# GateLoop attention and a gated layer on one core: scores, states' sums and value products of two chunks grouped by kind, and a guard's ScalarE part behind x's upper half

## The chip, the cores and the metric

The kernel runs on one core of a Trainium2 chip. The metric is the time of one execution on the device, in microseconds (us); lower is better. The core has engines that work side by side, each in the order of its own queue: TensorE (PE in the profile; PEld is its loading of weights), VectorE (DVE), ScalarE (ACT), GpSimd (POOL) and SyncE (SP, which here only issues DMAs).

## The reference

For each of 4 batches and 8 heads a complex state of 48 x 48 runs through 768 time steps; the output of each step is the query times the state's real part. The outputs of all heads are put side by side to x (3072 tokens x 384), and x goes through a layer of width 2048.

```python
mag = np.sqrt(a_re * a_re + a_im * a_im)
scale = np.minimum(mag, 0.999) / (mag + 1e-06)
a_re_n, a_im_n = (a_re * scale, a_im * scale)
for t in range(S):
    new_re = ar * S_re - ai * S_im            # ar, ai: step t of a_re_n, a_im_n
    new_im = ar * S_im + ai * S_re
    kv = np.einsum('bhd,bhe->bhde', k[:, :, t], v[:, :, t])
    S_re, S_im = (new_re + kv, new_im)
    y[:, :, t] = np.einsum('bhd,bhde->bhe', q[:, :, t], S_re)
...
h = x @ w_in
g = h * np.cos(h)
return (g @ w_out).astype(np.float32)
```

q, k, v, a_re and a_im have the shape (4, 8, 768, 48); w_in is 384 x 2048 and w_out 2048 x 384. All is float32.

## The kernel before, in words

The recurrence is computed in chunks of 128 steps. The gates' logarithms and angles are summed up within a chunk by matmuls with triangular matrices (`lgs` for the logarithms, `phs` for the angles); keys and queries are turned and scaled by them (`ks`, `qs`; transposed they are `kT`, `qT`). Then a chunk needs three kinds of matmul: the scores `sc` (keys by queries, 8 heads, in two halves), which VectorE multiplies by a causal mask into `atm`; the chunk's own contribution to the state, `sp` (values by keys), from which VectorE makes the next chunk's `state` in two steps (`state<-sp,state`, then `state<-state,end`; at the start of a batch one step, `state<-sp,end`); and the value products `yp`, which add `atm` times values and `state` times queries. ScalarE copies `yp` to `yT`, from where x goes to memory and comes back as `xT`.

The 24 chunks are taken in 12 groups g0 to g11 of two chunks. A batch has three groups, so g3, g6 and g9 begin a batch (chunk 1 has no state to read) and g2, g5, g8 and g11 end one (their chunk 2 makes no state). The main loop runs over the groups from g2 on; one turn, a stage here, does the attention of group n, the preparation of gates, keys and queries for group n+1, the hidden layer of group n (`hp`, `hb`: x by w_in, with the cosine on ScalarE and products on VectorE into `gate`), and the products with w_out of group n-1 (`sum`, `op`; VectorE makes combinations of gates, `s` and `t_s` tiles, for them, and `ot` collects the output). For some of the w_in tiles x is split in an upper and a lower part: `xh` (ScalarE, `x_halves.upper`), `xl` and `xx` (VectorE, `lower` and `apart`).

A stage's order is written by a function `weave`. Each entry is a list of steps with two numbers, and the steps are emitted in the order of numbers spread evenly between the two:

```python
weave((mixes(n - 1, 1, 2), 0.0, 0.08), (logs(n + 1), 0.0, 0.02), (chunks(n), 0.0, 0.36),
      ...
      (products(n - 1, 1, 2), 0.05, 0.24), ...
```

The matmuls keep the order in which they are emitted; each is chained to the one before. The vector and scalar operations of the stages are then placed by a scheduler when the kernel is built, so their order in the queues follows from the emitted order and from what they need. `behind(a, b)` forbids that a is placed ahead of b. PSUM tiles of the kinds `sc`, `sp`, `yp`, `lgs`, `phs` and `hb` share five buffers.

`chunks(n)` emits for each chunk in turn the scores, the state's sums and its steps (`f_state`), and the value products (`f_out`); in the middle of chunk 2's `f_out` stands a call, `between`, that emits the matmuls `lgs` of the next group (`prods`). Behind chunk 2 come the store of x, loads of `im` and `v` and x's transposed load. `products(n-1, 1, 2)` are the `op` matmuls of one part of the group before. `guard` looks, on ScalarE, at pieces of the raw weights that POOL's queue fetches into the places of `kT` and `qT` (tile `raw`): an Abs, then a Relu with an accumulated sum; two guards run in each stage from g3 on, and each stands behind the last scalar operation emitted so far (`tail["scalar"]`).

In the profile almost all matmuls carry the line of one helper (L692), and most vector and scalar operations that of a wrapper (L681); L712 is a helper for ScalarE's function calls, L733 the one that makes `hi`, the upper part of a float.

Of the kernel before, what the change touches and what calls it, by code (L numbers as in the profile page):

```python
# [18 lines left out]
AF = mybir.ActivationFunctionType  # L19
# [468 lines left out]
def fast_path(ctx, tc, q, k, v, a_re, a_im, moe_w_in, moe_w_out, out, least, odd, wide,  # L488
# [11 lines left out]
    NCH = S // C  # L500
    G = 2
    N = B * NCH
    NG = N // G
# [30 lines left out]
    late = {}  # L534
    tail = {}
# [7 lines left out]
    def behind(ins, other):  # L543
        tc.add_manual_dep(ins.ins, other.ins.name, mybir.DependencyInfo(
            mybir.DependencyClass.NoSync, mybir.DependencyReason.DATA))
# [82 lines left out]
    def fetched(src, home=None):  # L628
        _, a, b = src.shape
        pool, tag = (ft, home) if home else (stage["pool"], "raw")  # L630
        raw = pool.tile([C, a, b], I64, tag=tag, name="raw", bufs=stage["bufs"])
        chain(nc.gpsimd.dma_start(out=raw, in_=src), "gpsimd")
        words = raw.rearrange("p a b -> p (a b)").bitcast(U32).rearrange(
            "p (a b two) -> p a b two", a=a, two=2)
        return words[:, :, :, 0], words[:, :, :, 1]
# [9 lines left out]
        yield  # L645
        vector.tensor_tensor(out=bits, in0=bits, in1=lo, op=ALU.add)

    def guard(src, home):

        _, e = fetched(src, home)
        bits = e.bitcast(F32)
        behind(scalar.activation(out=bits, in_=bits, func=AF.Abs), tail["scalar"])
        scalar.activation(out=bits, in_=bits, func=AF.Relu, scale=-1.0, bias=least_e_b,
                          accum_out=odd[:, ds(next(odds), 1)])

# [368 lines left out]
    def f_scores(n, hh):  # L1026
        y, (g, i) = Y[n], divmod(n, G)
        if i == 0 and hh == 0:
            X[g]["atm"] = ft.tile([C, G, H, C], F32, tag="atm", name="atm", bufs=1)
        y["atm"] = X[g]["atm"][:, i]  # L1030
        ps = pa.tile([C, HH, C], F32, tag="a", name="sc")
        for h in range(HH):
            head = hh * HH + h
            matmul(ps[:, h], lhsT=X[n // G]["kT"][:, n % G * H + head],
                   rhs=queries(n, head), start=True, stop=True)
        y["masked"] = vector.tensor_tensor(
            out=y["atm"][:, ts(hh, HH)], in0=ps, in1=causal.unsqueeze(1).to_broadcast([C, HH, C]), op=ALU.mult)
        if "whole" in X[n // G - 1]:
            behind(y["masked"], X[n // G - 1]["whole"])

    def f_out(n, between=lambda: None):
        y, (g, i) = Y[n], divmod(n, G)
        vals = X[g]["v"][:, i]
        state = y.get("state")
        if i == 0:
            X[g]["yT"] = ft.tile([C, HH, G, C], F32, tag="yT", name="yT", bufs=1)
        ps = pa.tile([C, HH, C], F32, tag="a", name="yp")
        for p in range(HH):
            if p == (0 if n % NCH < NCH - 1 else 2):
                between()  # L1050
            for side in range(2):
                matmul(ps[ds(side * 64, D), p], lhsT=vals[:, 2 * p + side],
                       rhs=y["atm"][:, 2 * p + side], start=True, stop=(state is None))
            if state is not None:
                for side in range(2):
                    matmul(ps[ds(side * 64, D), p], lhsT=state[:, 2 * p + side],
                           rhs=queries(n, 2 * p + side), start=False, stop=True)
        for side in range(2):
            half = ds(side * 64, D)
            copied = scalar.copy(out=X[g]["yT"][half, :, i], in_=ps[half])  # L1060
            if g >= PEG:
                behind(copied, late["upper"])
# [58 lines left out]
    def f_state(n):  # L1121
        if n % NCH < NCH - 1:
            state_sums(n)
            for _ in state_next(n):
                pass

    def f_x(g, i=0, n=G):

        if i == 0:
            X[g]["moved"] = rows_d.tile([HH, 2, D, G, C], F32, tag="x", name="x")  # L1130
        for side in range(2):
            late["x"] = nc.sync.dma_start(
                out=X[g]["moved"][:, side, :, ds(i, n)].rearrange("p d g t -> d p g t"),
                in_=X[g]["yT"][ds(side * 64, D), :, ds(i, n)])
# [47 lines left out]
    def x_halves(g):  # L1182

        x = X[g]

        def all_of():
            return x["xT"].rearrange("p c g t -> p (c g t)")

        def upper():
            for name, tag in ("xx", "lg"), ("xh", "lo"), ("xl", "rs"):  # L1190
                x[name] = gt.tile([C, G * DM], F32R, tag=tag, name=name)

            scalar.activation(out=x["xh"], in_=all_of(), func=AF.Copy, scale=1.0 - 2.0 ** -13)

        def lower():
            rest_ = vector.tensor_tensor(out=x["xl"], in0=all_of(), in1=x["xh"].bitcast(F32),
                                         op=ALU.subtract)
            if g + 1 < NG:
                behind(rest_, X[g + 1][BEFORE])

        def apart():
            x["apart"] = vector.scalar_tensor_tensor(
                out=x["xx"], in0=x["xl"].bitcast(F32), scalar=-SHIFT,
                in1=x["xh"].bitcast(F32), op0=ALU.mult, op1=ALU.add)

        return upper, lower, apart
# [226 lines left out]
    def mixes(g, lo, hi):  # L1433
        return [lambda p=p: mixed(g, p) for p in range(lo, hi)] if g >= PLAIN else []
# [34 lines left out]
    def prods(g):  # L1469
        return powers(g) if 0 <= g < NG else []  # L1470
# [11 lines left out]
    def logs(g):  # L1482
        yield from each(g_log, g)
# [7 lines left out]
    def phases(g):  # L1491
        return [lambda i=i: g_phase(g, i) for i in range(G)] if 0 <= g < NG else []

    def chunks(g):
        for n in range(g * G, g * G + G):
            for hh in range(2):
                yield lambda n=n, hh=hh: f_scores(n, hh)
            yield lambda: None
            yield lambda n=n: (f_state(n), f_out(n, lambda: n % G and [t() for t in prods(g + 1)]))
        yield lambda: (f_x(g), g + 2 < NG and load(g + 2, ("im",), put=after_x), f_xt(g))  # L1500
        if PEG < g + 1 < NG:
            yield lambda: (ends(g + 1), load(g + 1, ("v",), put=lambda **kw: behind(
                nc.sync.dma_start(**kw), late["ends"])))
        if g + 2 < NG:
            late["next"] = [lambda: load(g + 2, ("k", "q"), put=turned_first)]
# [29 lines left out]

    def guarded(homes):

        for home, _ in zip(homes, list(guards)):
            yield lambda home=home: guard(guards.pop(0), home)

    into, back = weight_parts()
    guards = [src for _, src in into + back if src.dtype != F32]
# [277 lines left out]
    for n in range(2, NG):  # L1820
        turned_keys, plain = list(keys(n + 1)), n == PLAIN
        split = x_halves(n) if any(three(n, jp) for jp in THREE) else ()
        guard_ = list(guarded(("kT", "qT"))) if n > 2 else []
        convert = [lambda jp=jp: halves(jp) for jp in THREE if FROM[jp] == n + 1]
        weave((mixes(n - 1, 1, 2), 0.0, 0.08), (logs(n + 1), 0.0, 0.02), (chunks(n), 0.0, 0.36),
              (upper[2:] if plain else [], 0.0, 0.2), (products(n - 1, 0, 1), -0.02, -0.01),
              (products(n - 1, 1, 2), 0.05, 0.24), (products(n - 1, 2, 3) if n < NG - 1 else [], 0.28, 0.36),
              (mixes_again(n - 1, "s3"), 0.06, 0.18), (mixes_again(n - 1, "s2"), 0.19, 0.27),
              (angles(n + 1), 0.2695, 0.2699), (carries(n + 1), 0.336, 0.34), (second(n - 1, 1), 0.36, 0.5),
              (mixes_again(n - 1, "s4"), 0.37, 0.48),  # L1830
              (products(n - 1, 2 + (n < NG - 1), 7), 0.4, 0.56),
              (convert[0:-2], 0.76, 0.76), (convert[-2:], 0.76, 0.98),
              (phases(n + 1), *((0.472, 0.476) if plain else (0.476, 0.484))),
              (turned_keys[0:1], 0.5, 0.5), (split[0:1], *[0.54 if n < NG - 1 else 0.525] * 2), (turned_keys[1:2], 0.53, 0.53),
              (turned_keys[2:3], 0.56, 0.56), (turned_keys[3:4], 0.6, 0.6), ([lambda: rest_of(n - 1)], 0.605, 0.605), (split[1:2], *[0.542 if n < NG - 1 else 0.53] * 2),
              (split[2:3], *[0.544 if n < NG - 1 else 0.54] * 2), ([lambda: p_end(n + 1, 0, G)] if n + 1 < NG else [], 0.615, 0.615), (last_quarter() if plain else [], 0.9, 1.0), (first(n), 0.56, 1.0),
              (mixes(n, 0, 1), 0.98 if convert else 0.92, 1.0 if n < NG - 1 else 0.97), (guard_[0:1], 0.47, 0.47),
              (guard_[1:2], 0.505, 0.505))
    checked = verdict(late, temp)

    def judged():
# [99 lines left out]
```

## Time and profile before

| | before |
|---|---|
| median of 3 runs | 629.77 us (629.24 to 630.23) |
| profiled execution, whole | 629.86 us |
| its span in the profile | 628.1 us, 12990 instructions |
| PE busy | 608.1 us (97%) |
| PEld busy | 555.3 us (88%) |
| DVE busy | 531.8 us (85%) |
| ACT busy | 461.3 us (73%) |
| POOL busy | 28.5 us (5%) |
| DMA | 95.04 MB, mean 151 GB/s |

The span is what the engines' records cover; about 1.8 us of the execution lie outside it. Busy shares are averages over the whole span: what an engine's wait costs is read in the stage where it stands. A row of the timeline gives the start in us, the duration, engine, line, operation, `out<-in`, shapes and the number of records run together (a matmul in this number format leaves two records; `x16` is eight matmuls); in square brackets stands the idle time before it and what ended that. Neighbouring operations of an engine overlap at their edges, so what one costs in a row of them is read from start to start.

### The profile page before, as it was taken

What the parts mean: (1) busy time and instruction counts of PE and PEld (TensorE: products, weight loads), DVE (VectorE), ACT (ScalarE), POOL (GpSimd) and SP (SyncE); (2) the same over time, 40 slices, a digit from 0 to 9 for tenths busy, and PEclk for the clock granted to TensorE, in tenths of its full rate; (3) what the DMA queues carried; (4) which work ended last, traced back from release to release, by engine and by line L of the source; (5) the groups of instructions that cost most, each with busy time, mean ns of one, the idle gap of its engine ahead of it and who ended that gap; (6) DMA issues with size and microseconds to landing.
All of it is one profiled execution on the core that took longest, in us unless ns stands there. A gap on an engine that the chain in (4) does not pass through costs nothing.

```text
span 628.1 us, 12990 instructions
## 1 busy us (share of the span) xinstructions
PE 608.1 (97%) x5057; PEld 555.3 (88%) x5057; DVE 531.8 (85%) x779; ACT 461.3 (73%) x832; POOL 28.5 (5%) x45
## 2 busy tenths in 40 slices
PE   8899999999999998998999999999999999999995
PEld 5788867776889998998999999998999999999995
DVE  6999989967898799899889989889889989982471
ACT  7888687286698597698598698598599598572440
POOL 4010110000000000000000000000000000000000
PEclk9999999999999999999999999999999999999999
DMA  9969574714937567486396496496496494371001
GB/s 235 257 185 226 166 214 79 201 46 107 226 69 187 152 148 202 125 180 176 102 223 179 111 220 175 105 218 166 121 222 174 110 228 125 104 176 52 27 0 32
DMA packets 237569, 95.04 MB, mean 151 GB/s; under 512 B 209501, under 2 KB 229726, under 8 KB 237498
## 3 DMA queue, kind: packets, MB, share of 16 engines
q1 hardware_dynamic: 229960, 68.51, 46.5%
q0 software_dynamic: 5824, 25.50, 13.1%
q8 instruction: 42, 0.69, 0.5%
q10 hardware_dynamic: 1714, 0.11, 0.2%
q14 instruction: 29, 0.24, 0.1%
HBM read 69.28 MB, written 24.81 MB: 150 GB/s over the span
## 4 chain that ended last, share of the span: by engine, by line
PE 55%; ACT 19%; DVE 13%; issue 5%; DMA 4%; SPq 2%; ACTq 0%; DVEq 0%
PE hp L692 20%; PE op L692 13%; PE sum L692 12%; PE hb L692 3%; ACT xT L681 2%; PE yp L692 2%; DVE tr L681 2%; PE phs L692 2%; ACT tan L712 2%; ACT rs L712 2%; ACT gate L712 2%; DMA kT<-moved 2%; ACT L708 2%; ACT lg L712 2%; DVE gate L681 2%
## 5 line engine op out<-in xcount | busy, mean ns | idle before, releaser
L712 ACT ACTIVATE gate<-hp,half_pi_b 128x512 f32<-128x512 f32 x96 | 68.7, 715 | 50.2 <-PE hp L692 30.3
L692 PE MATMUL hp<-xT,w_in 128*128 128x256 f32 (+1 forms) x492 | 104.9, 369 | 0.0
L692 PE MATMUL op<-w_out,gate 128*128 128x192 f32 (+1 forms) x464 | 102.3, 370 | 0.0
L692 PEld LDWEIGHTS hp<-xT,w_in 128*128 128x128 f32 x492 | 89.7, 190 | 12.6 <-issue 0.2
L692 PEld LDWEIGHTS op<-w_out,gate 128*128 128x128 f32 x464 | 78.7, 190 | 15.2 <-issue 0.4
L692 PE MATMUL hp<-xh,wh 128*128 128x256 f32 x342 | 60.8, 286 | 0.0
L681 ACT ACTIVATE xT<-hp 128x512 bf16<-128x512 f32 x96 | 60.0, 625 | 0.0
L692 PE MATMUL hp<-xl,wl 128*128 128x256 f32 x342 | 59.0, 281 | 0.0
L692 PE MATMUL sum<-w_out,gate 128*128 128x192 f32 x304 | 52.5, 326 | 0.0
L681 DVE SCALAR_TENSOR_TENSOR gate<-hp,gate 128x512 f32<-128x512 f32 x57 | 39.2, 688 | 13.0 <-ACT xT L681 12.7
L692 PE MATMUL sc<-qT,kT 96*128 96x128 f32 x384 | 49.6, 278 | 0.3 <-ACT qT L681 0.3
L692 PEld LDWEIGHTS hp<-xh,wh 128*128 128x128 f32 x342 | 49.5, 189 | 0.5
L692 PEld LDWEIGHTS sc<-qT,kT 96*128 96x128 f32 x384 | 46.7, 192 | 3.2 <-issue 1.9
L692 PEld LDWEIGHTS sum<-w_out,gate 128*128 128x128 f32 x304 | 49.5, 190 | 0.1
L692 PE MATMUL hb<-xx,wx 128*128 128x256 f32 x342 | 48.6, 282 | 0.0
L692 PEld LDWEIGHTS hp<-xl,wl 128*128 128x128 f32 x342 | 48.4, 188 | 0.0
L681 DVE TENSOR_TENSOR hp<-hp,gate 128x512 f32<-128x512 f32 x57 | 39.3, 693 | 6.8 <-PE hp L692 2.6
L692 PEld LDWEIGHTS hb<-xx,wx 128*128 128x128 f32 x342 | 44.0, 188 | 0.0
L681 ACT ACTIVATE gate<-hb 128x512 f32<-128x512 f32 x57 | 35.8, 628 | 10.8 <-PE hb L692 9.8
L692 PE MATMUL yp<-atm,v 128*48 128x128 f32 x352 | 33.8, 278 | 3.4 <-DVE atm L681 3.4
L681 DVE TENSOR_TENSOR gate<-hp,gate 128x512 f32<-128x512 f32 x39 | 26.2, 678 | 12.8 <-ACT xT L681 12.6
L681 DVE TENSOR_TENSOR atm<-sc,causal 128x512 f32<-128x512 f32 x48 | 32.3, 683 | 4.8 <-PE sc L692 4.8
(161 smaller groups left out, 1222.2 us busy)
## 6 DMA issues: line engine op xcount, KB each, us to landing
moved<-tr SPq DMA_DIRECT2D x20, 768.0 KB
raw<-in_moe_w_in_dram POOLq DMA_DIRECT2D x16, 768.0 KB, 5.7
raw<-in_moe_w_out_dram POOLq DMA_DIRECT2D x16, 768.0 KB, 5.3
kT<-moved SPq DMA_DIRECT2D x80, 96.0 KB
qT<-moved SPq DMA_DIRECT2D x20, 384.0 KB
k<-in_k_dram SPq DMA_DIRECT2D x24, 192.0 KB
q<-in_q_dram SPq DMA_DIRECT2D x24, 192.0 KB
v<-in_v_dram SPq DMA_DIRECT2D x24, 192.0 KB
```

Source lines behind the costliest of these rows:

```text
L681: ins = getattr(self.engine, op)(**kw)
L692: chain(nc.tensor.matmul(out, **kw), "tensor")
L708: chain(nc.scalar.preload_act_table_set(table))
L712: chain(nc.scalar.activation(func=func, **kw))
```

## The change

`chunks(n)` is split into four entries: `scores(n)` for both chunks, then `states(n)` for both, then `outs(n)` (value products of both, then the x store, the `im` loads and x's transposed load), and later `fetches(n)` (`v` and `k`, `q` loads). The call in the middle of `f_out` is gone, and `prods(n+1)` has an entry of its own. `products(n-1, 1, 2)` has a narrower place. `guard` is split into the raw piece's fetch and the ScalarE part; the second guard's ScalarE part now stands behind `xh`, and the fetches and ScalarE parts have a place each. The number of matmuls, vector and scalar operations and loads is the same.

```diff
-    def guard(src, home):
-        _, e = fetched(src, home)
+    def guard(raw, other):
+
+        _, e = raw
         bits = e.bitcast(F32)
-        behind(scalar.activation(out=bits, in_=bits, func=AF.Abs), tail["scalar"])
+        behind(scalar.activation(out=bits, in_=bits, func=AF.Abs), other)
...
-    def f_out(n, between=lambda: None):
+    def f_out(n):
...
-            if p == (0 if n % NCH < NCH - 1 else 2):
-                between()
...
-            scalar.activation(out=x["xh"], in_=all_of(), func=AF.Copy, scale=1.0 - 2.0 ** -13)
+            late["xh"] = scalar.activation(out=x["xh"], in_=all_of(), func=AF.Copy,
+                                           scale=1.0 - 2.0 ** -13)
...
-    def chunks(g):
-        for n in range(g * G, g * G + G):
-            for hh in range(2):
-                yield lambda n=n, hh=hh: f_scores(n, hh)
-            yield lambda: None
-            yield lambda n=n: (f_state(n), f_out(n, lambda: n % G and [t() for t in prods(g + 1)]))
+    def own(g):
+        return range(g * G, g * G + G)
+
+    def scores(g):
+        return [lambda n=n, hh=hh: f_scores(n, hh) for n in own(g) for hh in range(2)]
+
+    def states(g):
+        return [lambda n=n: f_state(n) for n in own(g)]
+
+    def outs(g):
+        for n in own(g):
+            yield lambda n=n: f_out(n)
         yield lambda: (f_x(g), g + 2 < NG and load(g + 2, ("im",), put=after_x), f_xt(g))
+
+    def fetches(g):
...
+        raws = {}
         for home, _ in zip(homes, list(guards)):
-            yield lambda home=home: guard(guards.pop(0), home)
+            yield lambda home=home: raws.update({home: fetched(guards.pop(0), home)})
+            yield lambda home=home: guard(raws[home], tail["scalar"] if home == homes[0] else late["xh"])
...
-        weave((mixes(n - 1, 1, 2), 0.0, 0.08), (logs(n + 1), 0.0, 0.02), (chunks(n), 0.0, 0.36),
+        weave((mixes(n - 1, 1, 2), 0.0, 0.08), (logs(n + 1), 0.0, 0.02), (scores(n), 0.0, 0.05), (states(n), 0.05, 0.06), (outs(n), 0.06, 0.09),
+              ([lambda: [t() for t in prods(n + 1)]], 0.13, 0.13), (fetches(n), 0.342, 0.342),
...
-              (products(n - 1, 1, 2), 0.05, 0.24), (products(n - 1, 2, 3) if n < NG - 1 else [], 0.28, 0.36),
+              (products(n - 1, 1, 2), 0.1, 0.15), (products(n - 1, 2, 3) if n < NG - 1 else [], 0.28, 0.36),
...
```

On TensorE, this is the middle of g7's attention before: the end of chunk 1's value products, then chunk 2 (a row's number of matmuls stands behind the `x`).

```order
L692 MATMUL yp<-qT,state 48x128 x2
L692 MATMUL sc<-qT,kT 128x128 x4
L692 MATMUL op<-w_out,gate 128x192 x4
L692 MATMUL sc<-qT,kT 128x128 x4
L692 MATMUL sp<-v,ks 32x48 x24
L692 MATMUL lgs<-hi,exact 128x384
L692 MATMUL lgs<-lo,exact 128x384
L692 MATMUL lgs<-hi,exact 128x384
L692 MATMUL lgs<-lo,exact 128x384
L692 MATMUL yp<-atm,v 48x128 x2
L692 MATMUL yp<-qT,state 48x128 x2
```

Now g7's attention begins with these rows on TensorE (the last two repeat for the other heads):

```order
L690 MATMUL sum<-w_out,gate 128x192 x8
L690 MATMUL sc<-qT,kT 128x128 x16
L690 MATMUL sp<-v,ks 32x48 x48
L690 MATMUL yp<-atm,v 48x128 x2
L690 MATMUL yp<-qT,state 48x128 x2
```

and it ends with these:

```order
L690 MATMUL yp<-atm,v 48x128 x2
L690 MATMUL yp<-qT,state 48x128 x2
L690 MATMUL op<-w_out,gate 128x192 x4
L690 MATMUL lgs<-hi,exact 128x384
L690 MATMUL lgs<-lo,exact 128x384
L690 MATMUL lgs<-hi,exact 128x384
L690 MATMUL lgs<-lo,exact 128x384
L690 MATMUL op<-w_out,gate 128x192 x4
```

Between chunk 1's and chunk 2's value products stood half of the scores, four `op` matmuls, an `sp` and `lgs`; now nothing stands between them, and both groups of `op` and `lgs` follow.

On VectorE, the same stage before, from the first combination of gates behind the first mask:

```order
L681 TENSOR_TENSOR s<-gate 128x512
L681 TENSOR_TENSOR atm<-sc,causal 128x512
L681 TENSOR_TENSOR gate<-gate 128x4x128
L681 SCALAR_TENSOR_TENSOR pair<-re,pair 128x768
L681 TENSOR_SCALAR lg<-lg 128x768
L681 SCALAR_TENSOR_TENSOR state<-sp,state 96x384
L681 TENSOR_TENSOR lg<-lg,rs 128x768
L681 TENSOR_TENSOR state<-state,end 96x384
L681 TENSOR_TENSOR gate<-s,gate 128x4x128
L681 SCALAR_TENSOR_TENSOR lo<-lg,hi 128x768
L681 TENSOR_TENSOR atm<-sc,causal 128x512
L681 SCALAR_TENSOR_TENSOR ot<-op,ot 128x192
```

And now on VectorE, from the first mask on:

```order
L679 TENSOR_TENSOR atm<-sc,causal 128x512 x2
L679 TENSOR_TENSOR s<-gate 128x512
L679 SCALAR_TENSOR_TENSOR pair<-re,pair 128x768
L679 TENSOR_TENSOR atm<-sc,causal 128x512
L679 TENSOR_SCALAR lg<-lg 128x768
L679 TENSOR_TENSOR atm<-sc,causal 128x512
L679 TENSOR_TENSOR lg<-lg,rs 128x768
L679 SCALAR_TENSOR_TENSOR state<-sp,state 96x384
L679 TENSOR_TENSOR gate<-gate 128x4x128
L679 SCALAR_TENSOR_TENSOR lo<-lg,hi 128x768
L679 TENSOR_TENSOR state<-state,end 96x384
L679 TENSOR_TENSOR gate<-s,gate 128x4x128
```

All four masks and `lo` stand ahead of the second step of the state (`state<-state,end`), where two masks stood ahead of it and two masks and `lo` behind it.

On ScalarE, in g7's hidden-layer phase before (`rs<-rs` is the cosine that ends the preparation of keys, and the two `raw` rows are the second guard):

```order
L712 ACTIVATE rs<-rs,half_pi_b 128x768
L681 ACTIVATE raw<-raw 128x768
L681 ACTIVATE raw,odd<-raw,least_e_b 128x768
L681 ACTIVATE ot<-sum 128x192
L681 ACTIVATE xh<-xT 128x768
```

And now:

```order
L710 ACTIVATE rs<-rs,half_pi_b 128x768
L679 ACTIVATE xh<-xT 128x768
L679 ACTIVATE raw<-raw 128x768
L679 ACTIVATE ot<-sum 128x192
L679 ACTIVATE raw,odd<-raw,least_e_b 128x768
```

`xh` has moved ahead of the second guard.

More of the change, by code (lines that the diff above doesn't have):

```diff
@@ L1836, in fast_path @@
               (split[2:3], *[0.544 if n < NG - 1 else 0.54] * 2), ([lambda: p_end(n + 1, 0, G)] if n + 1 < NG else [], 0.615, 0.615), (last_quarter() if plain else [], 0.9, 1.0), (first(n), 0.56, 1.0),
-              (mixes(n, 0, 1), 0.98 if convert else 0.92, 1.0 if n < NG - 1 else 0.97), (guard_[0:1], 0.47, 0.47),
-              (guard_[1:2], 0.505, 0.505))
+              (mixes(n, 0, 1), 0.98 if convert else 0.92, 1.0 if n < NG - 1 else 0.97), (guard_[0:2], 0.47, 0.4701),
+              (guard_[2:3], 0.505, 0.505), (guard_[3:4], 0.541, 0.541))
     checked = verdict(late, temp)
```

## The prediction

> **What bounds the kernel now.** I read the engine shares first, then PE's idle time by releaser, then the stretch of each stage that the change rewrites, then the three engines row by row in one stage.
>
> ```profile
> PE 608.1 (97%) x5057; PEld 555.3 (88%) x5057; DVE 531.8 (85%) x779; ACT 461.3 (73%) x832; POOL 28.5 (5%) x45
> PEclk9999999999999999999999999999999999999999
> PE yp L692 <- DVE atm L681: 3.4, 4, 1.1
> PE lgs L692 <- DVE lo L681: 1.6, 3, 0.8
> ```
>
> TensorE (PE) is busy 97% of 628.1 us, and its longest wait in the attention part is 1.1 us: time is lost only where PE can be made to wait, and can be won only from waits and matmuls. The change rewrites, in each stage g, the stretch from the first score matmul to the first `sum` on a `t_s` tile. These are the stretches of g2 to g11, in order (us, then PE, PEld, DVE, ACT, POOL busy, PEclk, DMA share, GB/s):
>
> ```profile
> 126.29:142.06 15.77, 14.74 (x166) 11.43 (x164) 10.84 (x15) 13.48 (x24) 0.00 (x0) 1.00 0.18 53
> 176.84:189.92 13.08, 12.23 (x198) 10.81 (x196) 13.03 (x21) 12.89 (x21) 0.75 (x1) 1.00 0.21 61
> 226.04:240.23 14.19, 13.12 (x215) 11.70 (x213) 13.73 (x23) 14.00 (x23) 0.74 (x1) 1.00 0.43 106
> 276.31:289.61 13.30, 12.17 (x165) 10.88 (x164) 13.16 (x21) 13.12 (x22) 0.74 (x1) 1.00 0.39 89
> 324.83:337.31 12.48, 12.18 (x197) 10.76 (x197) 12.48 (x20) 12.29 (x21) 0.74 (x1) 1.00 0.61 150
> 371.77:384.55 12.78, 12.78 (x213) 11.68 (x213) 12.67 (x21) 12.53 (x21) 0.71 (x1) 1.00 0.56 132
> 419.43:432.57 13.14, 12.18 (x165) 10.89 (x165) 13.03 (x21) 11.69 (x21) 0.71 (x1) 1.00 0.57 140
> 466.89:479.12 12.23, 12.16 (x198) 10.81 (x197) 12.23 (x20) 12.04 (x21) 0.71 (x1) 1.00 0.58 139
> 513.57:526.35 12.78, 12.78 (x213) 11.68 (x213) 12.66 (x21) 12.54 (x22) 0.71 (x1) 1.00 0.50 112
> 561.23:572.30 11.07, 11.07 (x161) 10.24 (x160) 8.03 (x14) 1.99 (x5) 0.00 (x0) 1.00 0.09 32
> ```
>
> Here, from g3 to g10, VectorE (DVE) and often ScalarE (ACT) are as busy as PE: any order that puts PE ahead of DVE turns into a PE wait. Of 130.82 us only 5.4 are PE idle, so better overlap has little to win. Between two such stretches, in the hidden-layer phase, PE runs full:
>
> ```profile
> 337.31:371.77 34.46, 34.46 (x243) 33.98 (x242) 30.70 (x42) 26.57 (x52) 0.76 (x1) 1.00 0.70 176
> ```
>
> PE in g7's stretch (two records to a matmul, so x16 is eight):
>
> ```profile
> 371.77 1.95 PE L692 MATMUL sc<-qT,kT 96*128 96x128 f32 x16
> 373.55 1.47 PE L692 MATMUL op<-w_out,gate 128*128 128x192 f32 x8
> 374.95 0.88 PE L692 MATMUL sp<-v,ks 128*32 128x48 f32 x48
> 375.76 0.42 PE L692 MATMUL yp<-atm,v 128*48 128x128 f32 x4
> 377.66 1.16 PE L692 MATMUL sc<-qT,kT 96*128 96x128 f32 x8
> 378.65 1.47 PE L692 MATMUL op<-w_out,gate 128*128 128x192 f32 x8
> 379.96 1.05 PE L692 MATMUL sc<-qT,kT 96*128 96x128 f32 x8
> 381.75 0.44 PE L692 MATMUL lgs<-hi,exact 128*128 128x384 f32 x1
> 382.65 0.43 PE L692 MATMUL yp<-atm,v 128*48 128x128 f32 x4
> 382.91 0.39 PE L692 MATMUL yp<-qT,state 96*48 96x128 f32 x4
> 384.55 0.43 PE L692 MATMUL sum<-t_s,gate 128*128 128x192 f32 x1
> ```
>
> Start to start: scores of a chunk 1.78 us, the `op` groups 1.40 and 1.31, `sp` 0.81, a `yp` 1.90, `lgs` 0.90. DVE and ACT in the same stretch:
>
> ```profile
> 371.94 0.95 DVE L681 TENSOR_TENSOR lg<-lg,tan 128x768 f32<-128x768 f32 x1
> 374.01 0.68 DVE L681 TENSOR_TENSOR atm<-sc,causal 128x512 f32<-128x512 f32 x1
> 374.61 0.69 DVE L681 TENSOR_TENSOR s<-gate 128x512 f32<-128x512 f32 x1
> 376.41 0.96 DVE L681 SCALAR_TENSOR_TENSOR pair<-re,pair 128x768 f32<-128x768 f32 x1
> 377.27 0.56 DVE L681 TENSOR_SCALAR lg<-lg 128x768 f32<-128x768 f32 x1
> 377.74 0.55 DVE L681 SCALAR_TENSOR_TENSOR state<-sp,state 96x384 f32<-96x384 f32 x1
> 378.21 0.95 DVE L681 TENSOR_TENSOR lg<-lg,rs 128x768 f32<-128x768 f32 x1
> 379.08 0.55 DVE L681 TENSOR_TENSOR state<-state,end 96x384 f32<-96x384 f32 x1
> 380.34 0.96 DVE L681 SCALAR_TENSOR_TENSOR lo<-lg,hi 128x768 fp32r<-128x768 f32 x1
> 374.23 0.33 ACT L681 ACTIVATE ot<-sum 128x192 f32<-128x192 f32 x1
> 375.42 0.85 ACT L712 ACTIVATE pair<-lg 128x768 f32<-128x768 f32 x1
> 379.48 0.83 ACT L733 ACTIVATE hi<-lg 128x768 fp32r<-128x768 f32 x1
> ```
>
> Here chunk 2's first matmul on the state starts at 382.91, and the state was ready at 379.08 + 0.55 = 379.63: 3.3 us of slack. That slack came from the scores of chunk 2, the `op`s, `sp` and `lgs` that stood in between.
>
> **The change, part by part.**
>
> *Order on PE.* Now both chunks' scores stand first (2 x 1.78 = 3.56), then both `sp` (1.62), then chunk 1's `yp` (1.90), then chunk 2's. Its first four matmuls read only masks (0.26, from 382.65 to 382.91), so the state is wanted at 3.56 + 1.62 + 1.90 + 0.26 = 7.3 us after the first score, where it was 11.14 before. Where a batch ends (g5, g8, g11) one `sp` is missing: 6.5. Where it begins (g3, g6, g9) chunk 1 has no state to read and its `yp` is shorter by 0.86: 6.4. All `op`s and `lgs` now stand behind the `yp`s and cover nothing.
>
> *Order on DVE.* Ahead of the second step of chunk 1's state (`state<-state,end`) there now stand `lg`, two `gate`s, two masks, `s`, `pair`, a mask, the scaled `lg`, a mask, `lg`, the first state step, `gate` and `lo`. Against before these are two masks and `lo` more: 2 x 0.60 + 0.88 = 2.08 us, so 379.08 becomes 381.16. In full, by g7's steps from start to start (512-wide 0.60, 768-wide 0.87 or 0.86, `lo` 0.88, the scaled `lg` and a state step 0.47): from `lg` at 371.94, `s` ends at 375.81; `pair` waits for ACT's `pair<-lg`, which ended at 375.42 + 0.85 = 376.27 and, with ACT's small `ot` copy now two places later, ends about 0.23 earlier, so `pair` starts near 376.15. Then 0.86 + 0.60 + 0.47 + 0.60 + 0.87 + 0.47 + 0.60 + 0.88 = 5.35 (ACT's `hi`, which `lo` needs, ends near its old 380.31 and in time) brings the second state step to 381.50 and its end to 382.05: S = 10.28 after the first score, against 7.3 wanted. PE waits 3.0 us. Behind the waiting matmul stand the rest of `yp` (1.90 - 0.26 = 1.64), 1.40, 0.90 and 1.31, together 5.25, all in PE's queue. The stretch takes S + 5.25 = 15.53 for 12.78.
>
> The other stages by the same sum with their own rows; S and the change of the stretch: g4 9.74, +0.8; g5 9.59, +1.5; g6 8.60, +1.4; g7 10.28, +2.75; g8 10.10, +2.2; g9 8.01, +1.0; g10 10.31, +2.8: together +12.5. In g2, g3 and g11 the state comes about in time (S 9.43, 7.07, 6.57) and old waits go: -1.0, -0.75, -0.15. Sum +10.6. The differences between stages come mostly from the batch position (a new batch's first state needs one step and not two) and from conversions of weights on ACT and DVE at the start of g4 and g5.
>
> *Fewer changes of matmul kind.* Eight score records took 0.99 between others and 0.89 within a run of 16, so a change of kind costs about 0.10; some four fewer in a stage. This is inside the sums.
>
> *The guard.* Its two ACT operations stood ahead of `xh`; now the second guard's stand behind. In g7's hidden-layer phase:
>
> ```profile
> 399.31 0.95 DVE L681 TENSOR_TENSOR qs<-pair,rs 128x768 f32<-128x768 f32 x1
> 400.86 0.96 DVE L681 TENSOR_TENSOR xl<-xT,xh 128x768 fp32r<-128x768 f32 x1 [0.60 <-ACT xh L681]
> ```
>
> DVE waits 0.60 for `xh`; with `xh` some 2 us earlier it is held by `qs` alone, and gains 0.60. ACT does the same work in another order and gains nothing by itself. PE does not wait in this phase, so the gain shows only if DVE and ACT are still that much earlier when the next stage's scores begin. They run back to back for most of the phase, so I take the gain as passed on to S of g6 to g10 (0.6 each, -3.0 in all); in g4 and g5 DVE waits for PE at the start, and I take nothing. Ends of this term: 0 and -3.0. The guard's DMA on POOL keeps its place and its tile is free as before: nothing.
>
> *Moved loads and stores.* Chunk 2's `yT` copies on ACT, the store of x, `im`, `v` and `ends` move within the stage. Their readers are in the hidden-layer phase or a stage later; SP's queue gets the x store and the `im` loads ahead of the `re` pieces. Cover: the ~34 us phase. If a load were late, `lg` of the next stage would be, and S with it. I take 0, ends -0.5 and +1.5 (a wait as long as PE's longest, in one or two stages).
>
> Sum: +10.6 - 3.0 = +7.6 on the profiled execution's 629.86 (span 628.1, the rest lies outside it), about 637.4; the median of the runs is 629.77, so I say 637.3, 1.2% slower.
>
> **Rivals.**
>
> *The state is in time, and it is faster.* If DVE delivers the state before PE wants it, all waits in the stretch vanish: 3.56 + 1.62 + 3.80 + 1.40 + 0.90 + 1.31 = 12.59 in g4, g7, g10, 0.81 less in g5 and g8, 0.86 less in g3, g6, g9. Against the rows: -2.0, -2.9, -2.6, and about -1.5 in g2 and g11: -9.0, so 620.8. For it: DVE's wait for `xh` goes. Against: from `lg` to the state DVE alone has 9.8 us of steps, so it would have to begin 2.5 us before the first score, where in g7 it began 0.17 after. It decides in steps: each microsecond by which S is earlier in g4 to g10 is worth about 7 us, so no change comes at S 1.1 us earlier than summed, in all seven stages.
>
> *About no change:* such a partial lead, between 628.5 and 631.
>
> *The guard's 0.6 us does not reach the next stage:* +10.6, 640.4. For it: ACT, not DVE, ends last at `pair`, and ACT does no less. Against: ACT waits for DVE's and PE's tiles in the phase.
>
> *The clock drops in the stalls.* All forty slices show a granted clock in the top tenth, and no wait in the stretches passes 1.1 us; waits of 2 to 3 us are new to this kernel. The trace cannot exclude that they lower it. If each of the five longest stalls put 3.4 of the 5.25 us behind it at half speed, each would cost 1.7 more, together 8.5: 645. Against: no row shows a clock that falls. The Trainium skill states such a rule in "TensorE: Matmul & The Clock Gate", Part 1: the clock falls to half after an idle window of about 3.4 us, and comes back after as long a busy one. By that rule the stalls summed here (3.0 us in g7 and 3.6 in g8, both without the guard's gain) stand at the edge; no run so far shows it in this kernel.
>
> **How the numbers follow.** Forecast with the guard's gain (637.3) 0.5, without it (640.4) 0.3, with the clock (645) 0.05; no change 0.07; faster 0.08. What a measurement can tell from no change here is 0.2%, 1.26 us. So faster 0.08, same 0.07, slower 0.85. The range: at the top 640.4 with +1.5 for a late load and 1 for steps read by hand, 643; at the bottom, S 0.9 us earlier than summed in the seven stages, 6.3 less, 631. Outside lie the clock (0.05), the faster case (0.08) and no change (0.07).
>
> **What would show it.** Right: PE's idle list gains a row for `yp` waiting for DVE's `state`, some 7 times, 15 to 20 us in all, the longest near 3; the stretches of g7 and g10 grow to 15 us and g3 does not grow; the `xl <- xh` wait on DVE is gone; PE's wait of `lgs` for `lo` goes. Wrong: no such row, or stretches near 12.6. If the stretches grow and the time does not, PE had slack in the phase between, which I saw nowhere. If the wait is for `atm` instead, the masks were mis-sized and not the state.

## The result, and the profile after

The changed kernel takes 637.98 us (median of 4 runs, 635.99 to 639.27) where before takes 630.0 (629.24 to 630.99): a ratio of 1.0123, 95% interval 1.0092 to 1.0154. It is slower, by 8 us against 7.5 forecast. The profiled execution is the fastest of the four, 635.99 us with a span of 634.0, 5.9 more than before's span. From its page, and from PE's idle time by releaser (us, times, longest):

```profile
PE 605.3 (95%) x5057; PEld 559.5 (88%) x5057; DVE 532.7 (84%) x779; ACT 460.9 (73%) x832; POOL 28.8 (5%) x45
PEclk9999999999999999998999999999999999999999
PE yp L690 <- DVE state L679: 16.0, 9, 3.0
PE sum L690 <- ACT ot L679: 0.9, 2, 0.5
PE yp L690 <- DVE atm L679: 0.3, 1, 0.3
```

The first line of waits is new: PE waits 16.0 us, nine times, for the state. The old waits of `yp` for masks and of `lgs` for `lo` are nearly gone. The PEclk line has an 8 that before did not have. In each stage PE stands still at the same matmul, chunk 2's first on the state (here g2 to g10 in order):

```profile
135.38 0.42 PE L690 MATMUL yp<-qT,state 96*48 96x128 f32 x4 [0.19 <-DVE state L679]
182.31 0.43 PE L690 MATMUL yp<-qT,state 96*48 96x128 f32 x4 [0.66 <-DVE state L679]
233.88 0.43 PE L690 MATMUL yp<-qT,state 96*48 96x128 f32 x4 [2.44 <-DVE state L679]
284.43 0.67 PE L690 MATMUL yp<-qT,state 96*48 96x128 f32 x4 [2.96 <-DVE state L679]
334.42 0.43 PE L690 MATMUL yp<-qT,state 96*48 96x128 f32 x4 [1.25 <-DVE state L679]
383.35 0.43 PE L690 MATMUL yp<-qT,state 96*48 96x128 f32 x4 [2.30 <-DVE state L679]
432.18 0.42 PE L690 MATMUL yp<-qT,state 96*48 96x128 f32 x4 [2.87 <-DVE state L679]
479.01 0.43 PE L690 MATMUL yp<-qT,state 96*48 96x128 f32 x4 [1.08 <-DVE state L679]
527.94 0.43 PE L690 MATMUL yp<-qT,state 96*48 96x128 f32 x4 [2.30 <-DVE state L679]
```

The stretches of g3 to g10, from the first score to the first `sum` on a `t_s` tile, as before:

```profile
175.19:187.39 12.20, 11.54 (x198) 10.91 (x197) 11.97 (x19) 11.99 (x18) 1.50 (x2) 1.00 0.33 96
224.10:238.96 14.86, 12.43 (x215) 11.80 (x214) 14.37 (x24) 14.64 (x24) 1.50 (x2) 1.00 0.44 104
274.81:292.49 17.68, 14.72 (x166) 13.88 (x165) 15.36 (x23) 14.82 (x25) 1.49 (x2) 0.81 0.47 122
326.71:339.50 12.79, 11.54 (x198) 10.91 (x198) 12.46 (x20) 12.51 (x21) 1.50 (x2) 1.00 0.59 133
373.71:388.43 14.72, 12.42 (x214) 11.79 (x213) 14.10 (x22) 12.40 (x21) 1.42 (x2) 1.00 0.68 167
422.65:437.26 14.61, 11.74 (x166) 11.12 (x166) 13.46 (x20) 12.49 (x22) 1.42 (x2) 1.00 0.56 126
471.47:484.09 12.62, 11.54 (x198) 10.91 (x197) 12.62 (x20) 12.40 (x22) 1.42 (x2) 1.00 0.70 167
518.30:533.02 14.72, 12.42 (x214) 11.79 (x213) 14.09 (x22) 12.39 (x21) 1.42 (x2) 1.00 0.55 128
```

Together they take 114.20 us for 103.98, 10.2 more. One row differs from the others in its PEclk column: g5 had a granted clock of 0.81. The half of that stretch behind the wait shows it plainly (8.06 us where the same matmuls take 5.08 in g7, from 383.35 to 388.43):

```profile
284.43:292.49 8.06, 8.06 (x49) 7.66 (x49) 5.74 (x8) 5.33 (x11) 0.75 (x1) 0.61 0.37 97
```

So 3.0 us of the 5.9 are a clock that fell at the wait of 2.96 us, and 2.9 us are everything else. Outside the stretches of g3 to g10 time was won: 0.35 by g2's first score, 1.3 in stage g2, 2.6 in the hidden-layer phases (from g5 on they take 34.21 or 34.22 us, where before had 34.32 to 35.22; g3's is 0.6 longer), and 0.1 at the end.

### The profile page after: what moved, and what is told of

Its sections match the earlier page's. It is cut to its first block, busy times and chain, and to the rows that moved or that the text cites. A ratio compares the mean times of both kernels' runs of the same rounds, so it can differ in the third digit from the quotient of the medians.

```text
span 634.0 us, 12973 instructions
## 1 busy us (share of the span) xinstructions
PE 605.3 (95%) x5057; PEld 559.5 (88%) x5057; DVE 532.7 (84%) x779; ACT 460.9 (73%) x832; POOL 28.8 (5%) x45
## 4 chain that ended last, share of the span: by engine, by line
PE 64%; DVE 17%; ACT 12%; issue 3%; SPq 2%; DMA 1%; DVEq 0%; ACTq 0%
PE hp L690 20%; PE op L690 18%; PE sum L690 13%; PE yp L690 3%; PE hb L690 3%; ACT gate L710 2%; DVE lg L679 2%; DVE gate L679 2%; PE phs L690 2%; ACT xT L679 2%; DVE tr L679 2%; DVE atm L679 2%; ACT L706 2%; PE busy L690 2%; DVE pair L679 1%
## 5 line engine op out<-in xcount | busy, mean ns | idle before, releaser
L690 PE MATMUL op<-w_out,gate 128*128 128x192 f32 (+1 forms) x464 | 104.1, 376 | 0.0
L690 PEld LDWEIGHTS op<-w_out,gate 128*128 128x128 f32 x464 | 80.4, 192 | 16.9 <-issue 1.8
L690 PE MATMUL yp<-qT,state 96*48 96x128 f32 x304 | 31.0, 282 | 16.0 <-DVE state L679 16.0
L690 PE MATMUL sc<-qT,kT 96*128 96x128 f32 x384 | 45.5, 276 | 0.3 <-ACT qT L679 0.3
L690 PEld LDWEIGHTS sc<-qT,kT 96*128 96x128 f32 x384 | 44.5, 192 | 1.0 <-ACT qT L679 0.5
L679 ACT ACTIVATE ot<-sum 128x192 f32<-128x192 f32 x39 | 12.6, 323 | 36.7 <-PE sum L690 35.4
```

Source lines behind the costliest of these rows:

```text
L679: ins = getattr(self.engine, op)(**kw)
L690: chain(nc.tensor.matmul(out, **kw), "tensor")
```

## Experiments

The theory: PE waits for the state as summed, and the longest of these waits lower the clock, which costs more. The rivals named in the expectations: the clock is noise, the guard does it, or VectorE is the bound of these stretches, so that a wait taken away comes back at the next place.

**The changed kernel again (after_again).** No edit.

> The changed kernel as it is, once more, to see how its time goes with its granted clock. Theory A (PE waits for the state some 16 us in nine stages, and the longest of these waits lower PE's clock in some stages for some 3 us more): the runs spread over 635 to 640 us and the higher times have the lower mean clock, about 1 us for each 0.001; the waits for the state are 16.0 us in every run. Rival R (the stalls cost all of it, the clock is noise): times do not go with the clock, and lie within 1 us.

Measured: 638.1 us (6 runs, 636.76 to 639.04), ratio 1.0123 (1.0100 to 1.0146). The waits for the state are 16.2 us, for 16.0 in the first trace. Over the ten runs of this kernel, those with a mean clock of 0.993 took 635.99 to 637.72 us, and those with 0.986 to 0.991 took 637.50 to 639.27. So the times go with the clock, but a line through the ten gives 0.34 us for each 0.001, not the 1 us that theory A had. In this trace the parts behind the waits of g5 (2.97), g8 (2.89) and g10 (2.31) are long: from the `yp` on the state to the `sum`, 7.81, 6.71 and 6.56 us for 5.08, together 5.8 us. Its span of 636.8 less 5.8 is 631.0; the first trace's 634.0 less 3.0 is 631.0 too. Two executions that differ by 2.8 us agree once the clock is taken out.

**The guard alone (guard_only).** Before, with the change's three hunks on `guard`, `guarded` and `xh`, and their numbers.

> The order of before, with only the guard split and its second ScalarE part behind xh. Theory A: VectorE's wait for xh goes (7.4 us before, now under 2) but PE has 3.3 us of slack for the state in this order, so only part of the 5.4 us of PE waits in the stretches goes: 628 to 629.5 us. Rival: PE is full in the hidden-layer phase and nothing reaches it, 630.0 within 0.6.

Measured: 628.23 us against 629.82, ratio 0.9974 (0.9956 to 0.9992): a little faster, as theory A had it. But its reason is only in part there. VectorE's wait of `xl` for `xh` was to fall below 2 us, and the tile view of `xl` has

```profile
ACT xh L679: 5.3, 8
```

where before had 7.4, 8. In g7 ScalarE now waits 1.55 us for a `sum` ahead of `xh`. The state is ready 7.55 us after g7's first score, for 7.86 in before: the edit alone is worth 0.3 us there, and PE does not wait for the state in this order.

**The order alone (order_only).**

```diff
-            yield lambda home=home: guard(raws[home], tail["scalar"] if home == homes[0] else late["xh"])
+            yield lambda home=home: guard(raws[home], tail["scalar"])
...
-              (guard_[2:3], 0.505, 0.505), (guard_[3:4], 0.541, 0.541))
+              (guard_[2:4], 0.505, 0.5051))
```

> The changed order of matmuls, with the guard where it was. Theory A: the state comes 0.6 us later in g6 to g10, so PE waits for it 19 us in all for 16.0, the longest 3.4 to 3.6 in g8 for 2.9, and the clock drops in more stages: 641 to 647 us. Rival (the guard's gain of before does not reach the next stage): waits 16 us, 638 as the changed kernel.

Measured: 637.81 us, ratio 1.0126 (1.0100 to 1.0152), waits for the state 16.1 us, the longest 3.0. That is the changed kernel, and theory A's 641 to 647 is wrong. The guard's edit makes no difference that can be measured in the new order. The 0.6 us for which I gave it credit is there without it. ScalarE's timeline in g7 shows where `xh` stands:

```profile
402.42 0.92 ACT L679 ACTIVATE raw<-raw 128x768 f32<-128x768 f32 x1
403.22 0.84 ACT L679 ACTIVATE xh<-xT 128x768 fp32r<-128x768 f32 x1
403.95 1.02 ACT L679 ACTIVATE raw<-raw,least_e_b 128x768 f32<-128x768 f32 x1
```

With the new order of matmuls the scheduler puts `xh` between the guard's two operations by itself, and in g7 VectorE's `xl` no longer waits (0.8 us are left in the whole trace, in two waits). Whether this is what brings the state 0.6 us earlier is not shown: in g7's stretch VectorE's `pair` waits 0.33 us for ScalarE (0.32 in the changed kernel), so ScalarE sets the time there.

**Idle matmuls in the waits (fill, fill_fit).** The changed kernel and, ahead of chunk 2's value products,

```diff
+        if i and g in (4, 5, 7, 8, 10):
+            idle_ = pa.tile([C, HH, C], F32, tag="a", name="idle")
+            for _ in range(30):
+                matmul(idle_[:, 0], lhsT=exact, rhs=exact, start=True, stop=True)
```

> The changed kernel with 30 matmuls of 128 x 128 more, which nobody reads, ahead of chunk 2's value products in g4, g5, g7, g8 and g10, where PE waits longest. Theory A: they fill about 1.7 us of each wait, the wait for the state falls from 16.0 to about 8 us, the state comes when it came, and the clock stays near 0.998: 633 to 635 us and a spread under 1 us, faster than the changed kernel by doing more. Rival R: nothing is gained by filling a wait, 638 us or more, with the clock as low as before.

Measured: 638.91 us (636.03 to 642.20), ratio 1.0135 (1.0099 to 1.0170), no verdict on the theory. I had guessed 0.06 us for such a matmul, and they took 0.113: 3.4 us in each wait, 0.4 to 1.1 more than the waits hold, 4.1 us in all. Three runs had a clock of 0.997 or 0.998 (636.03 to 637.65) and three of 0.990 to 0.992; the trace has its fall at 33.8 us, ahead of the stages that the idle matmuls are in. Of the 58 runs of before that stand beside these experiments, seven have a clock of 0.987 to 0.994 too and take 632.45 to 636.75 us; no trace shows where it fell in them. So the number was fitted: 20, 24, 18, 23 and 18 matmuls.

> As fill, with as many idle matmuls as the wait holds at the measured 0.113 us each: 20 in g4, 24 in g5, 18 in g7, 23 in g8, 18 in g10. The 30 of fill took 3.4 us in waits of 2.3 to 3.0 and so cost about 4 us. Theory A (the long waits lower the clock): the wait for the state falls from 16 to 4 or 5 us, no stretch shows a lower clock, and the time is that of the changed kernel without its clock loss, 633.0 within 0.8, some 5 us faster than the changed kernel. Rival R (the clock drop is not from the waits): 637 to 639.

Measured: 632.79 us (9 runs, 632.16 to 633.65), ratio to before 1.0045 (1.0031 to 1.0060). The clock is 0.997 to 0.999 in every run. From its page, its waits, and g5:

```profile
PEclk9999999999999999999999999999999999999998
PE yp L690 <- DVE state L679: 3.0, 4, 1.1
281.26 2.89 PE L690 MATMUL idle<-exact 128*128 128x128 f32 x24
289.59 2.76 PE L690 MATMUL sum<-t_s,gate 128*128 128x192 f32 x16
```

A kernel that does 103 useless matmuls more is 5.2 us faster than the one without them (4.9 by their ratios to before), because PE does not stand still there: all nine runs keep the clock, where the ten of the changed kernel have 0.986 to 0.993. The trace's span, 631.2 us, is that of the changed kernel's two traces less their clock losses (631.0). So of the 8 us by which the changed kernel is slower, 5 are the clock and 3 the waits less what the order won elsewhere. The clock was no noise.

**Work in the waits (op_between).**

```diff
-              (products(n - 1, 1, 2), 0.1, 0.15), (products(n - 1, 2, 3) if n < NG - 1 else [], 0.28, 0.36),
+              (products(n - 1, 1, 2), 0.066, 0.074), (products(n - 1, 2, 3) if n < NG - 1 else [], 0.28, 0.36),
```

> The changed kernel with the eight op matmuls of products(n-1,1,2) between chunk 1's and chunk 2's value products (numbers 0.066 to 0.074 for 0.1 to 0.15). They read gates that are long ready and take 2.7 us, as long as the longest waits but one. Theory A: the waits for the state fall from 16 to about 1 us, no clock loss, 633.0 - 15.5 = 617.5, with 616 to 621 for waits that take their place. Rival R (the order by kinds itself costs, through VectorE being the bound of these stretches): the waits come back at lgs, sum or phs, and the time is that of before, 627 to 630.

Measured: 628.27 us, ratio 0.9978 (0.9953 to 1.0003). Not distinguishable from before, and 10.8 us above theory A's 617.5. PE's waits, then g7's stretch and what follows it:

```profile
PE sum L690 <- ACT ot L679: 6.5, 7, 1.6
PE sum L690 <- DVE gate L679: 1.3, 2, 1.0
369.92 3.74 PE L690 MATMUL sc<-qT,kT 96*128 96x128 f32 x32
382.47 2.76 PE L690 MATMUL sum<-t_s,gate 128*128 128x192 f32 x16
388.59 2.87 PE L690 MATMUL sum<-t_s,s 128*128 128x192 f32 x16 [0.76 <-ACT ot L679]
387.48 0.84 ACT L731 ACTIVATE hi<-tan 128x768 fp32r<-128x768 f32 x1 [0.68 <-DVE tan L679]
388.23 0.31 ACT L679 ACTIVATE ot<-sum 128x192 f32<-128x192 f32 x1
```

The stretch itself is short, 12.55 us (from 369.92 to 382.47; the prediction's faster rival had 12.59). But rival R is right that the wait came back: `sum` may not go on before ScalarE has copied it to `ot`, and that copy stands behind `hi`, which waits for VectorE. Against the changed kernel without its clock loss, the stretches of g3 to g10 are 12.8 us shorter and the phases behind them 7.6 longer. Rival R's reason (VectorE is the bound) is not decided by this: what is late is an order on ScalarE.

**The state sooner (state_first, both).** The logs' last steps get the number 0.0605, just behind the states, and

```diff
-        vector.tensor_tensor(out=m2, in0=m2, in1=rs, op=ALU.subtract)
+        less = vector.tensor_tensor(out=m2, in0=m2, in1=rs, op=ALU.subtract)
+        if g > PEG:
+            behind(less, late["state"])
```

where `late["state"]` is the last step of chunk 1's state.

> The changed order on PE, with VectorE's logarithm difference and lo placed behind the second step of chunk 1's state (the logs' last steps get the number 0.0605, and the difference is put behind the state). Theory A (0.87 + 0.88 us of VectorE work ahead of the state): the state comes 1.75 us earlier, the waits fall from 16 to about 5 us, the longest to 1.2, no clock loss: 622 to 625. Rival R: lgs waits for lo instead and takes it back, 630 or more.

Measured: 629.69 us (627.10 to 633.61, clock 0.988 to 0.997), ratio 1.0007 (0.9986 to 1.0028). The waits fell from 16 to 8.7 us and not to 5:

```profile
PE yp L690 <- DVE state L679: 8.7, 8, 2.7
284.40 0.67 PE L690 MATMUL yp<-qT,state 96*48 96x128 f32 x4 [2.69 <-DVE state L679]
380.99 0.43 PE L690 MATMUL yp<-qT,state 96*48 96x128 f32 x4 [0.56 <-DVE state L679]
```

In g7 the state came 1.73 us earlier (380.99 less the first score at 373.08 is 7.91, for 9.64), as summed. In g4 and g5 it came only 0.27 earlier, the waits stayed at 2.17 and 2.69, and the clock still fell at the second. There `lo` stood behind the state already, so the edit moved only the logarithm difference (0.87), and a combination of gates (0.60) took its place. Expected 622 to 625: a miss, by the clock and by those two stages. Rival R is not the reason: `lgs` waits for `lo` once, 0.3 us.

> op_between and state_first together. Theory A: the state is early by 1 us or more in all stages and no wait is left in the stretches except what lgs may wait for lo (up to 0.5 us a stage): 616 to 619, no faster than op_between by more than 1 us. Rival R: VectorE is the bound and it equals op_between whatever its value, or is slower by the lgs wait.

Measured: 629.66 us, ratio 0.9993 (0.9981 to 1.0006). No wait for the state is left, `sum` waits 6.8 us for `ot` and `lgs` 1.9 for `lo`. It is 1.4 us slower than op_between, about what rival R had for `lgs` waiting for `lo`, and slower than theory A's 616 to 619 mostly for op_between's reason.

**ScalarE's copy where ScalarE waits (ot_mid, ot_early).** op_between and

```diff
-(products(n - 1, 2, 3) if n < NG - 1 else [], 0.28, 0.36)
+(products(n - 1, 2, 3) if n < NG - 1 else [], 0.332, 0.34)
```

in ot_mid (0.272, 0.334 in ot_early).

> op_between with the matmuls of products(n-1,2,3) given the numbers 0.332 to 0.34 for 0.28 to 0.36, which leaves PE's order as it is and puts ScalarE's copy of sum to ot between the arctangent and hi, where ScalarE waits 0.68 us for VectorE's carry in any case. Theory A (in op_between the wait moved from the state to this copy, 6.5 us in seven stages, because the copy stands behind hi on ScalarE): PE's wait of sum for ot falls from 6.5 to under 1 us and the time falls by 5 to 7 us from op_between's 628.3: 621 to 623.5. Rival R (VectorE is the bound of the stage, and whatever wait is removed comes back at the next one): phs waits for hi or tan, and the time stays within 1.5 us of 628.3.

> The same with the numbers 0.272 to 0.334: the copy stands ahead of the function table's load, the arctangent and hi, where ScalarE has to wait for the sum itself. Theory A: the wait of sum for ot goes as in ot_mid, but the arctangent and hi come about 0.7 us later, which phs has slack for: 621 to 624. Rival R: phs waits for lo, 625 to 629.

Measured: ot_mid 620.07 us (618.59 to 620.61), ratio 0.9828 (0.9804 to 0.9851); ot_early 620.73, ratio 0.9851 (0.9829 to 0.9873). Faster than before by 1.7 and 1.5%, and than the changed kernel by 18 us. PE's waits of `sum` for `ot` are gone from both. In ot_mid these are left in the stretches, and ScalarE's copy stands so:

```profile
PE sum L690 <- DVE gate L679: 1.3, 2, 1.0
PE yp L690 <- DVE state L679: 0.2, 1, 0.2
381.28 0.84 ACT L710 ACTIVATE tan<-tan 128x768 f32<-128x768 f32 x1
382.03 0.31 ACT L679 ACTIVATE ot<-sum 128x192 f32<-128x192 f32 x1
382.81 0.84 ACT L731 ACTIVATE hi<-tan 128x768 fp32r<-128x768 f32 x1 [0.47 <-DVE tan L679]
```

The copy sits in ScalarE's own wait and costs it nothing: `hi` starts 17.56 us after g7's first score, as in op_between (387.48 less 369.92). Rival R falls here: VectorE did not bound the time at 628, it has the same work in a kernel that takes 620. The grouped order is 10 us faster than before's, once something that needs no state stands in front of the state's matmuls and the copy is not queued behind a wait. How much of this before's order would gain from the copy's move alone was not run; its waits of `sum` for `ot` are 1.8 us in all.

## Why the prediction was right, and where its steps were not

*When the state is wanted, and when it comes.* The prediction had 7.3 us after the first score for g7 and S = 10.28, or 9.65 with the guard's gain. Measured, PE came to a stand at 383.35 - 2.30 - 373.71 = 7.34 and went on at 9.64. S in g4 to g10, forecast with the gain: 9.74, 9.59, 8.0, 9.7, 9.5, 7.4, 9.7; measured 9.78, 9.62, 7.71, 9.64, 9.53, 7.54, 9.64. Waits forecast at 15 to 20 us, the longest near 3; measured 16.0 and 2.96. In-order arithmetic from the rows of before, with 0.6 us taken off for the guard in g6 to g10, held to 0.3 us in every stage.

*The work behind the wait.* Put at 5.25 us, it took 5.08: 1.2 us over seven stages.

*The guard.* Its size was right (0.6 us of S) and its cause wrong: order_only has the gain without the guard's edit. That the size came out is luck, and what makes the gain stays open. In before's order the edit is worth 1.6 us in the median (guard_only), not through the state.

*Outside the stretches nothing was to change.* This step failed, by 2.6 us in the hidden-layer phases of g3 to g10 and 0.35 ahead of g2. A steady phase takes 34.21 us for 34.32 and more. In g6 `sum`, `op`, `sum` at its start stand 0.10, 0.04 and 0.11 closer: the first `sum` stands behind an `op` now and not behind a `yp`, and a wait of 0.17 us for `ot` ahead of the last one's weight load is gone; what each of these is worth is not shown. PE's waits of `sum` for `ot`, 0.3 to 0.6 us in g4, g5, g7 and g10 of before, are gone too, all but one of 0.47 in g4, and g3 has a new one of 0.43.

*The sum.* Forecast +7.6 for the profiled execution; measured +2.9 without the clock. The difference is 1.2 (the tail), 0.3 (g6), 2.6 and 0.65 (the phases, the start and g2).

*The clock.* The rival with a chance of 0.05 happened, beside the forecast's waits: 3.0 us in the profiled execution, 5 in the median by fill_fit. Its price was put at 8.5 for five stages, 1.7 each; the falls seen cost 1.5 to 3.0 each, in one to three stages of an execution. So it is luck that the forecast of 637.3 came this close to 637.98: 4.7 us too much in the sum, most of it gains outside the stretches, stood against 5 us of clock that were left out of it. The likeliest case was right in its mechanism, the wait for the state, and 633 without the clock was inside the range.

*The faster rival.* It was priced at 620.8, for a state in time. ot_mid, where it is in time and nothing takes its place, takes 620.07. This agreement is partly luck too: ot_mid's stretches of g3 to g10 take about 2 us longer than that sum has them, and its phases about 3 us less than before's.

## What to carry to other kernels

Grouping matmuls of a kind takes away the work that hid another engine's latency; before doing it, write down when the first matmul behind the group wants its operand and add up, in order, what the other engine does until then. Independent work then belongs directly in front of that matmul, and the next wait has to be looked up at once: here it sat in a copy queued behind a waiting instruction, and moving it cost nothing. If no useful work can be had, a long wait on TensorE can be worth filling with matmuls that nobody reads: here filling five waits of 2.3 to 3.0 us took 5 us off, with waits of up to 1.07 us left as they were.

## What the runs showed of the hardware that was not expected

A wait of 2.3 to 3.0 us can lower TensorE's clock. Behind the wait of 2.96 in g5, four `yp` records run 0.43 us apart:

```profile
284.88 0.64 PE L690 MATMUL yp<-atm,v 128*48 128x128 f32 x4
285.31 0.64 PE L690 MATMUL yp<-qT,state 96*48 96x128 f32 x4
```

In g8 of after_again, where the clock has not fallen yet, they start 0.22 apart. That is half speed, and the granted clock says the same. These are stretches ahead of a fall and of the fall itself, for g5 and g8 of after_again (PEclk is the third number from the end):

```profile
279.93:283.34 3.41, 1.55 (x29) 1.29 (x24) 3.41 (x7) 3.34 (x5) 0.00 (x0) 1.00 0.74 229
283.34:290.17 6.83, 5.72 (x37) 5.32 (x37) 5.29 (x8) 4.95 (x9) 0.76 (x1) 0.50 0.13 29
430.11:433.52 3.41, 1.55 (x28) 1.49 (x28) 3.38 (x6) 2.34 (x5) 0.00 (x0) 1.00 0.21 87
433.52:436.94 3.42, 3.42 (x14) 3.23 (x11) 2.08 (x3) 1.16 (x2) 0.72 (x1) 0.50 0.52 84
```

The seven falls at waits for the state (one in the changed kernel's first trace, three in after_again, two in order_only, one in state_first) came at waits of 2.31 to 2.97 us. Each held half speed for 3.41 or 6.83 us and cost 1.5 to 1.6 or 2.7 to 3.0 us. The same waits fell in some executions and not in others: g8's 2.87 went without a fall in the first trace, its 2.89 had one in the second.

The traces show what makes the difference. The falls of one trace start whole multiples of 3.413 us apart (in after_again 150.18 and 245.76 us, 44 and 72 times it; in order_only 51.20, 15 times). If each of the four traces is cut from 10 to 600 us into windows of that length, beginning at one of its falls, the window just ahead of each of the seven falls holds 1.86 to 2.43 us of PE idle time, and no other window passes 1.81. So a wait costs clock when more than about 1.8 us of it lie in one window; this bound is an estimate from those windows. g8's 2.87 lay across two of them, 1.33 and 1.54.

One fall does not fit, and its cause stays open. In fill's trace the clock falls at 33.8 us behind a wait of 0.87, the only PE idle time in the window ahead:

```profile
30.38:33.79 3.41, 2.54 (x64) 2.35 (x64) 3.16 (x7) 3.37 (x5) 0.00 (x0) 1.00 0.99 257
33.79:40.62 6.83, 6.83 (x34) 6.83 (x33) 6.64 (x9) 5.22 (x7) 0.75 (x1) 0.50 0.67 176
```

The Trainium skill, "TensorE: Matmul & The Clock Gate", Part 1, has the clock fall to half after an idle window of about 3.4 us that runs freely; the half speed, the steps of 3.41 and 6.83 us and the chance from run to run agree with it, but the waits here were shorter than such a window, and the measurement decides: the prediction's reading, that waits of 3.0 stand at the edge, was too generous.
